# A two-layer decode kernel: the loads at the change of layers reordered, and one chunk of V more for VectorE

## The chip, the cores and the metric

The kernel runs on one core of a Trainium2 chip. The metric is the device time of one execution in microseconds (us). Three executions of the kernel before the change give a median; one further execution was recorded by the hardware profiler, and all rows below come from that one.

## The reference

One token passes twice through an attention block and an MLP, with the same weights and the same cache both times. Everything is float32.

```python
def A(x, k_cache, v_cache, wq, wo):          # D=512, 32 heads, 4096 positions, Dh=128
    q = (x @ wq).reshape(B, Sq, H, Dh).transpose(0, 2, 1, 3)
    scores = jnp.einsum("bhqd,bhkd->bhqk", q, k_cache) * (Dh ** -0.5)
    p = jax.nn.softmax(scores, axis=-1)
    o = jnp.einsum("bhqk,bhkd->bhqd", p, v_cache)
    return o.transpose(0, 2, 1, 3).reshape(B, Sq, H * Dh) @ wo

def B(x, w1, b1, w2, b2):                    # F=1376
    return jax.nn.gelu(x @ w1 + b1, approximate=True) @ w2 + b2

x = x + A(layernorm(x)); x = x + B(layernorm(x))
x = x + A(layernorm(x)); x = x + B(layernorm(x))
```

K and V of all heads are 67 MB each; layer two reads them again, less some blocks that stay on the chip from layer one.

## The kernel before, in words

**Tiling.** The 32 heads are eight groups of four (`G = 8`, `J = 4`). A group's K is one block of 8.4 MB (128 partitions x 16384 floats, eight chunks of 2048 columns, `NC`), and so is its V. Three homes of one block each in a big SBUF tile, `arena`, hold the blocks in turn (`RING` in layer one, `homes` in layer two); a smaller place, `PAIR`, takes the wo of a group and the wq of the next one (2.1 MB together). `SHARED`, inside one of the homes, takes w1 and w2 at the change of layers, and `SCRATCH` is its last 512 columns.

**Order.** Every large load is issued by SyncE's queue (`load`, line 80) in program order; one that waits for its home holds all behind it. TensorE's products are in program order too (`matmul`, line 84). A group goes: `scores` (32 products of 512 columns, which the profile counts as 64), `exponentials`, `weights`, then V. For the eleven groups that are not last or next to last in layer one nor the first two or the last in layer two, `partly` (line 379) gives the first `BY_PE` chunks of V to TensorE (`values`) and the others to VectorE (`weighted`, lines 242 and 247): one multiplication of all of them by their weights, then additions that halve the number of chunks until one is left. TensorE adds that one chunk up later (`sum_up`, line 253), at the head of the next `group`, ahead of the next scores. Behind those scores comes `out_product` with wo out of `PAIR`, and only when it has read `PAIR` may SyncE issue the next load of `PAIR`; the next K and V stand behind that load in the queue. Here is that order:

```python
        if ahead:
            t, rl, wt = ahead
            sum_up(t)
            on = head(rl)
        for c, t in k_blocks:
            scores(z, c, t)
        if ahead:
            out_product(on, wt)
```

**The change of layers.** Behind the last V of layer one comes `mlp` (line 283). Its w1 stands in four rows in `SHARED`; as each row has been used, `load_w2` puts a part of w2's eleven blocks of 512 columns over it. The last part, blocks 8 to 10, also covers `SCRATCH` and waits until line 300 has read it. After GELU the eleven blocks are multiplied one after the other (line 310), with an `idle` product (two passes of 512 columns that multiply zeros) behind blocks 1, 4, 7 and 10. Then `set_x` and `first_queries` begin layer two with the K of group 7, which is still there; wq of group 6 (`wq_t`, line 433) and the first units of group 6's K (`begin_k`) are loaded over w2's blocks, and more of that K over the chunks of `C_AT` as their scores are done. V of group 5 follows in two pieces into the same home; the second piece waits for `next_queries` of line 470.

**The end.** In layer two's last group K comes in two halves and V in four pieces; w1 and w2 go to `A_AT`, the home of the V block before, behind them in the queue.

Of the kernel before, what the change touches and what calls it, by code (L numbers as in the profile page):

```python
# [21 lines left out]
G = 8  # L22
# [3 lines left out]
FB = 11  # L26
W1C = FJ * J
EPS = 1e-5
U = 512
NC = 4 * U  # L30
# [9 lines left out]
SHARED = B_AT + KEPT_V  # L40
# [2 lines left out]
KEPT_K = PAIR + 2 * NC  # L43
ARENA = KEPT_K + U
HALVES = ((0, 4), (4, 8))
BY_PE = 3
W1_AT_END = ((0, 2), (2, 3), (3, 4))
LAST = ((0, 4), (4, 6), (6, 7), (7, 8))
W2_AT_CHANGE = ((0, 2), (2, 5), (5, 8), (8, 11))
W2_AT_END = ((0, 4), (4, 8), (8, 10), (10, 11))  # L50


# [1 line left out]
def decode_layers(ctx: ExitStack, tc: tile.TileContext, x, k, v, w, w1, b1, w2, b2, out):  # L54
# [10 lines left out]
    def small(name, n=1):  # L65
        if name not in places:
            a = sum(b - a for a, b in places.values())
            places[name] = a, a + n
        a, b = places[name]
        assert b <= 120 and b - a == n  # L70
        return smalls[:, a:b]
# [3 lines left out]
    def at(first, n):  # L75
        return arena[:, first : first + n]

    def load(first, src):
        t = at(first, src.shape[-1])
        tc.keep_in_program_order(nc.sync.dma_start(t, src))  # L80
        return t

    def matmul(*a, **kw):
        tc.keep_in_program_order(nc.tensor.matmul(*a, **kw))  # L84
# [7 lines left out]
    def of_w(row, i, n):  # L92
        return w[row][:, NC * i : NC * (i + n)]

    def by_four(t):
        return t.rearrange("p (j n) -> p j n", j=4)


    wq_t = by_four(load(SHARED, of_w(1, 0, 1)))
# [18 lines left out]
    pS, pO = (psum.tile([P, 512], F32, name=n) for n in ("pS", "pO"))  # L118
# [9 lines left out]
    def of_32(t, n, i=0):  # L128
        return t[:, : 32 * n].rearrange("p (c q) -> p c q", q=32)[:, :, i]
# [9 lines left out]
    def pairs(t):  # L139
        return t[:, :8].rearrange("p (c i) -> p c i", i=2)  # L140

    def turned(src, wide=False):

        t = work.tile([P, P], F32, name="turned")
        if wide:
            for j in range(J):
                q = slice(32 * j, 32 * j + 32)
                nc.vector.transpose(t[q], src[q, P * j : P * (j + 1)])  # L148
        else:
            nc.vector.transpose(t, src[:, :P])  # L150
        return t

    def set_x(xin0, scale, xin1, queries=True):
        s = small("x_sum")
        t = x_wide if queries else small("x1", 8)
        if not queries:
            nc.gpsimd.memset(pairs(t)[:, :, 1], 1.0)
        x = pairs(t)[:, :, 0]
        nc.vector.scalar_tensor_tensor(x, xin0, scale, xin1, op0=ALU.mult, op1=ALU.add, accum_out=s)
        if queries:  # L160
            for j in range(1, J):
                nc.gpsimd.tensor_copy(pairs(t[:, 32 * j :])[:, :, 0], x)  # L162
        return t, s

    def idle(to, n=U):
        matmul(to[:, :n], zero[:, 0:1].to_broadcast([P, P]), at(C_AT, n), start=True, stop=True)
# [6 lines left out]
    def mean_of(xs, s):  # L173
        nm = minus_mean(s, pS[:, 0:1])
        xc, sq, ss, negm = small("xc", 4), small("sq", 4), small("ss"), small("negm")
        nc.vector.tensor_scalar(xc, pairs(xs)[:, :, 0], nm, None, op0=ALU.add)
        nc.vector.scalar_tensor_tensor(sq, xc, 1.0, xc, op0=ALU.mult, op1=ALU.mult, accum_out=ss)
        nc.vector.tensor_copy(negm, nm)
        return negm, ss

    def rstd_of(ss):
        nv = minus_mean(ss, pS[:, 1:2])
        ve, r = small("ve"), small("rstd")
        nc.vector.tensor_scalar(ve, nv, -1.0, EPS, op0=ALU.mult, op1=ALU.add)
        nc.vector.memset(pS[:, 0:2], 0.0)
        nc.gpsimd.tensor_tensor(r, ve, power, op=ALU.pow)
        return r
# [43 lines left out]
    def values(i, pt, vt, c):  # L231
        for j in range(J):
            matmul(pO[32 * j : 32 * j + 4, :], pt[:, c, j, :], vt[j],
                   start=(i == 0), stop=(i == C - 1))
# [3 lines left out]
    def weighted(pt, home):  # L238
        first = home + NC * BY_PE
        t = at(first, NC * (C - BY_PE)).rearrange("p (n d) -> p n d", d=P)  # L240
        w = pt.rearrange("p c j b -> p (c j b)")[:, 4 * J * BY_PE :]
        nc.vector.tensor_tensor(t, t, w.unsqueeze(2).to_broadcast([P, 4 * J * (C - BY_PE), P]), op=ALU.mult)  # L242
        n = C - BY_PE
        while n > 1:
            m = n // 2
            a, b = at(first + NC * (n - 2 * m), NC * m), at(first + NC * (n - m), NC * m)
            nc.vector.tensor_tensor(a, a, b, op=ALU.add)  # L247
            n -= m
        return quarters(first)
# [30 lines left out]
            else:  # L280
                matmul(pO, on[:, d : d + P], wt[:, d, :], start=(d == 0), stop=(d == 3))

    def mlp(xs, s, w1_t, w2_t, load_w2=None):
        xb = small("xb", 4)
        nc.gpsimd.tensor_tensor(xb, pairs(xs)[:, :, 0], b2c, op=ALU.add)
        for c in range(4):
            for j in range(J):
                matmul(pO[32 * j : 32 * j + 2, :FJ], pairs(xs)[:, c, :], w1_t[c][:, FJ * j : FJ * (j + 1)],
                       start=(c == 0), stop=(c == 3))
            if c == 0:  # L290
                nm, ss = mean_of(xs, s)
            if c == 1:
                r = rstd_of(ss)
            if load_w2 and c < 3:
                load_w2(c)
        idle(pS)
        ht = at(SCRATCH, 32 * FB)
        nc.vector.transpose(ht, pO[:, : 32 * FB])  # L298
        h, u, a, z, t, g = (small(f"gelu_{i}", FB) for i in "huaztg")
        nc.vector.scalar_tensor_tensor(h, of_32(ht, FB, 1), nm, of_32(ht, FB), op0=ALU.mult, op1=ALU.add)  # L300
        if load_w2:
            load_w2(3)
        nc.vector.scalar_tensor_tensor(u, h, r, b1c, op0=ALU.mult, op1=ALU.add)
        nc.vector.scalar_tensor_tensor(a, u, 0.044715, u, op0=ALU.mult, op1=ALU.mult)
        nc.vector.scalar_tensor_tensor(z, a, 1.0, u, op0=ALU.add, op1=ALU.mult)
        nc.scalar.activation(t, z, AF.Tanh, scale=float(np.sqrt(2.0 / np.pi)))
        nc.vector.scalar_tensor_tensor(g, t, 1.0, u, op0=ALU.add, op1=ALU.mult)
        for c in range(FB):
            for j in range(J):
                matmul(pS[32 * j : 32 * j + 1, :P], g[:, c : c + 1], w2_t[c][:, P * j : P * (j + 1)],  # L310
                       start=(c == 0), stop=(c == FB - 1))
            if load_w2 and any(c == b - 1 for a, b in W2_AT_CHANGE):
                idle(pO)
        return of_32(turned(pS), 4), xb

    def load_w1(first, a, b):
# [2 lines left out]
    def load_w2(first, a, b):  # L319
        load(first + U * a, w2[:, U * a : U * b])  # L320

    def in_rows(first, n, rows):
        return [at(first + n * i, n) for i in range(rows)]
# [7 lines left out]
    xs, s = set_x(zero, 1.0, xcol)  # L331
# [19 lines left out]
    def next_queries(xs, negm, wt, to=pO):  # L351
        for c in range(4):
            wide_query_block(to, c, xs, wt)
        z = queries(to, negm, wide=True)
        if to is pS:
            nc.vector.memset(pS, 0.0)
        return z
# [21 lines left out]
    def partly(pt, v_blocks, home):  # L379
        for c, t in v_blocks:  # L380
            if c < BY_PE:
                values(c, pt, t, c)
# [6 lines left out]
    for g in range(G):  # L389
# [12 lines left out]
        for c, t in blocks(v, g, v_home, LAST if final else ((0, C),)):  # L402
# [3 lines left out]
            if g == G - 2:  # L406
                for j in range(J):
                    i = 4 * c + j - KEPT_V // U
# [8 lines left out]
        else:  # L417
            pair = load(PAIR, of_w(g % 2, g, 2))
            acc = add_up(acc, head_out(rl, by_four(pair[:, :NC])))
            wq_t = by_four(pair[:, NC:])  # L420
            z = next_queries(xs, negm, wq_t)
    x1, s1 = set_x(own, 1.0, acc, queries=False)
    own, xb = mlp(x1, s1, in_rows(SHARED, W1C, 4), in_rows(SHARED, U, FB),
                  lambda i: load_w2(SHARED, *W2_AT_CHANGE[i]))
    xs, s = set_x(own, 0.5, xb)


# [2 lines left out]
    g = G - 2  # L430
    negm, z, sc, nsc = first_queries(xs, s, wq_t)
    acc = pairs(xs)[:, :, 0]
    wq_t = by_four(load(SHARED, of_w((g + 1) % 2, g, 1)))
    k_t = []

    def begin_k(home, n):
        a = len(k_t)
        load(home, k[g][:, U * a : U * (a + n)])
        k_t.extend(at(home + U * i, U) for i in range(n))

    begin_k(SHARED + NC, 4)
    begin_k(SHARED + 2 * NC, 2)
    begin_k(PAIR + NC, 4)
    for c in range(C):
        scores(z, c, quarters(C_AT + NC * c))
# [27 lines left out]
    for n in range(2, G):  # L473
        g, final = G - 1 - n, n == G - 1
# [17 lines left out]
        own = head_out(rl, wo_t, last=True)  # L492
    x1, s1 = set_x(own, 1.0, acc, queries=False)
    own, xb = mlp(x1, s1, in_rows(A_AT, W1C, 4), in_rows(A_AT + 11 * U, U, FB))
    y = small("y", 4)
    nc.vector.scalar_tensor_tensor(y, own, 0.5, xb, op0=ALU.mult, op1=ALU.add)
# [43 lines left out]
```

## Time and profile before

| what | value |
|---|---|
| median of three executions | 678.74 us (677.17 to 679.43) |
| the profiled execution's own time | 680.62 us |
| its span, first to last instruction | 678.8 us |
| read from HBM | 285.88 MB, 421 GB/s over the span |
| mean granted TensorE clock | 0.796 of full speed |
| busy: TensorE, VectorE, ScalarE, GpSimd | 404.0, 333.1, 22.8, 4.3 us |

The own time is that of the execution that the profiler watched, so it holds 1.8 us outside of the span. Shares of busy time are means over stages that differ. A chain of waits, which goes back from the last instruction to what released each step, says which stage waits for what. In the rows, PE is TensorE, DVE is VectorE, ACT is ScalarE, POOL is GpSimd, and SPq is SyncE's queue; L84 is line 84.

### The profile page before, as it was taken

The numbers are of one execution on the slowest core, as the hardware profiler recorded it, in microseconds if no ns is written. First come the engines' busy times: TensorE is split into PE (matmuls) and PEld (weight loads), VectorE is DVE, ScalarE is ACT, GpSimd is POOL, SyncE is SP. The second block draws the span as 40 slices with busy tenths as digits, with TensorE's granted clock in tenths as the row PEclk, the third lists the DMA queues.
The fourth block names the chain that finished last, engine by engine and source line by source line (L and its number), as shares of the span: only waits on it lengthen the run. The fifth ranks groups of instructions, "written<-read, shape, count | busy, mean of one in ns | idle before, by whom it ended". The sixth has DMA issues, their size and how long they took to land.

```text
span 678.8 us, 5676 instructions
## 1 busy us (share of the span) xinstructions
PE 404.0 (60%) x2416; PEld 108.7 (16%) x2416; DVE 333.1 (49%) x489; ACT 22.8 (3%) x48; POOL 4.3 (1%) x21
## 2 busy tenths in 40 slices
PE   3533753638626566287688887647527465385586
PEld 1100210112101112021113222111102111121122
DVE  2059176393672936920211311295682945927622
ACT  0010000000000000001000110000000000000000
POOL 1000000000000000000000000000000000000000
PEclk9667785877759768688987998987668867778697
DMA  9999999999999999999999999999999999999996
GB/s 375 429 434 433 433 433 433 424 442 436 429 436 418 444 434 433 433 435 416 432 414 332 429 448 419 389 441 433 438 436 415 454 437 425 436 425 414 432 411 257
DMA packets 11402, 286.25 MB, mean 422 GB/s; under 512 B 1777, under 2 KB 1777, under 8 KB 3441
## 3 DMA queue, kind: packets, MB, share of 16 engines
q1 hardware_dynamic: 10944, 285.87, 98.6%
q8 instruction: 19, 0.31, 0.2%
q10 hardware_dynamic: 432, 0.01, 0.0%
q14 instruction: 7, 0.05, 0.0%
HBM read 285.88 MB, written 0.00 MB: 421 GB/s over the span
## 4 chain that ended last, share of the span: by engine, by line
DMA 57%; PE 31%; DVE 9%; issue 1%; SPq 1%; another core or an unknown queue 1%; ACT 0%; POOL 0%; DVEq 0%; ACTq 0%
DMA arena<-in_k 40%; PE pS L84 18%; PE pO L84 13%; DMA arena<-in_v 10%; DMA arena<-in_w 5%; DVE arena L242 3%; DVE arena L247 3%; DMA xcol<-in_x 1%; DVE turned L148 1%; SPq L80 1%; DVE arena L257 0%; ACT arena L214 0%; DVE ml L207 0%; DVE arena L298 0%
## 5 line engine op out<-in xcount | busy, mean ns | idle before, releaser
L84 PE MATMUL pS<-arena,zq 128*8 128x512 f32 x1024 | 136.9, 694 | 35.6 <-DMA arena<-in_k 31.7
L242 DVE TENSOR_TENSOR arena<-arena,turned 128x10240 f32<-128x10240 f32 x11 | 119.1, 10825 | 44.7 <-DMA arena<-in_v 44.7
L84 PE MATMUL pO<-arena,turned 128*4 128x512 f32 x584 | 93.3, 793 | 56.4 <-DMA arena<-in_v 54.8
L247 DVE TENSOR_TENSOR arena<-arena 128x2048 f32<-128x2048 f32 (+1 forms) x33 | 98.5, 2984 | 0.7
L84 PE MATMUL pO<-arena,one 128*4 128x512 f32 x88 | 20.8, 1037 | 127.1 <-DVE arena L247 127.1
L207 DVE TENSOR_REDUCE ml<-pS 128x1 f32<-128x512 f32 x16 | 11.1, 691 | 151.0 <-PE pS L84 151.0
L84 PE MATMUL pO<-arena,on_wide 128*128 128x512 f32 x112 | 51.8, 605 | 4.0 <-DVE on_wide L265 4.0
L84 PEld LDWEIGHTS pS<-arena,zq 128*8 128x8 f32 x1024 | 28.9, 99 | 150.4 <-issue 110.9
L84 PE MATMUL pS<-arena,x_wide 128*128 128x512 f32 x88 | 41.5, 614 | 3.6 <-DMA arena<-in_w 3.5
L257 DVE STREAM_TRANSPOSE arena<-pO 128x512 f32<-128x512 f32 x16 | 11.5, 716 | 56.3 <-PE pO L84 56.3
L84 PEld LDWEIGHTS pO<-arena,turned 128*4 128x4 f32 x584 | 16.1, 101 | 118.0 <-issue 112.4
L148 DVE STREAM_TRANSPOSE turned<-pO 32x128 f32<-32x128 f32 x72 | 22.3, 310 | 21.2 <-PE pO L84 20.4
L214 ACT ACTIVATE arena<-pS,mt,smalls 128x512 f32<-128x512 f32 x16 | 12.4, 777 | 494.9 <-DVE mt L212 494.8
L219 PE MATMUL pO<-ident,arena 128*128 128x128 f32 x64 | 10.5, 288 | 30.0 <-DVE turned L148 17.8
L84 PEld LDWEIGHTS pO<-arena,on_wide 128*128 128x128 f32 x112 | 20.1, 190 | 36.3 <-issue 29.5
L84 PE MATMUL pO<-arena,x_wide 128*128 128x512 f32 (+1 forms) x64 | 18.4, 477 | 9.5 <-POOL x_wide L162 6.7
L84 PEld LDWEIGHTS pO<-arena,one 128*4 128x4 f32 x88 | 1.2, 84 | 136.2 <-DVE arena L247 136.2
L84 PEld LDWEIGHTS pS<-arena,x_wide 128*128 128x128 f32 x88 | 16.3, 196 | 33.5 <-issue 16.9
L148 DVE STREAM_TRANSPOSE turned<-pS 32x128 f32<-32x128 f32 x44 | 13.7, 311 | 0.8
L219 PEld LDWEIGHTS pO<-ident,arena 128*128 128x128 f32 x64 | 6.8, 142 | 43.3 <-issue 27.4
L224 DVE STREAM_TRANSPOSE mt<-ml 128x32 f32<-128x32 f32 x16 | 3.4, 211 | 17.2 <-ACT arena L214 17.2
L84 PE MATMUL pO<-arena,smalls 128*2 128x344 f32 x64 | 8.2, 604 | 4.8 <-DMA arena<-in_w 4.1
(79 smaller groups left out, 121.5 us busy)
## 6 DMA issues: line engine op xcount, KB each, us to landing
arena<-in_w SPq DMA_DIRECT2D x13, 2048.0 KB, 11.5
arena<-in_k SPq DMA_DIRECT2D x4, 4096.0 KB, 24.5
arena<-in_v SPq DMA_DIRECT2D x2, 4096.0 KB, 38.4
arena<-in_w SPq DMA_DIRECT2D x6, 1024.0 KB, 20.2
arena<-in_v SPq DMA_DIRECT2D x3, 2048.0 KB, 42.8
arena<-in_v SPq DMA_DIRECT2D x1, 6144.0 KB, 26.2
arena<-in_w SPq DMA_DIRECT2D x6, 688.0 KB, 31.2
arena<-in_v SPq DMA_DIRECT2D x4, 1024.0 KB, 45.3
```

The source lines that it names most:

```text
L80: tc.keep_in_program_order(nc.sync.dma_start(t, src))
L84: tc.keep_in_program_order(nc.tensor.matmul(*a, **kw))
L148: nc.vector.transpose(t[q], src[q, P * j : P * (j + 1)])
L207: nc.vector.tensor_reduce(ml[:, 0:1], pS, axis=AX.X, op=ALU.max)
L214: nc.scalar.activation(p, pS, AF.Exp, bias=bias[:, 0:1], scale=sc, accum_out=ml[:, 0:1])
L219: tc.keep_in_program_order(nc.tensor.transpose(pT[:, b].rearrange("p j r -> p (j r)"), p[:, P * b : P * (b + 1)], ident))
L224: nc.vector.transpose(lt, ml)
L242: nc.vector.tensor_tensor(t, t, w.unsqueeze(2).to_broadcast([P, 4 * J * (C - BY_PE), P]), op=ALU.mult)
L247: nc.vector.tensor_tensor(a, a, b, op=ALU.add)
L257: nc.vector.transpose(ot, pO)
```

## The change

`BY_PE` goes from 3 to 2, so that VectorE takes six chunks of V where it took five. At the change of layers w2's last part is split into blocks 8 and 9 (issued when w1's last row has been used) and block 10 (issued behind line 300); wq is loaded in two halves behind blocks 1 and 3; the first two loads of K are issued behind blocks 7 and 9 instead of after `first_queries`; and the idle products behind blocks 1, 4, 7, 10 become idle products behind 4, 7, 9 and one of half the width behind 10.

```diff
-BY_PE = 3
+BY_PE = 2
-W2_AT_CHANGE = ((0, 2), (2, 5), (5, 8), (8, 11))
+W2_AT_CHANGE = ((0, 2), (2, 5), (5, 8), (8, 10), (10, 11))
...
-            if load_w2 and c < 3:
+            if load_w2:
                 load_w2(c)
...
         if load_w2:
-            load_w2(3)
+            load_w2(4)
...
-            if load_w2 and any(c == b - 1 for a, b in W2_AT_CHANGE):
-                idle(pO)
+            if load_w2:
+                behind_w2(c)
+                if c in (4, 7, 9):
+                    idle(pO)
+                elif c == FB - 1:
+                    idle(pO, U // 2)
...
+    def behind_w2(c):
+        if c in (1, 3):
+            load(SHARED + U * (c - 1), of_w((G - 1) % 2, G - 2, 1)[:, U * (c - 1) : U * (c + 1)])
+        if c == 7:
+            begin_k(SHARED + NC, 4)
+        if c == 9:
+            begin_k(SHARED + 2 * NC, 2)
+
     own, xb = mlp(x1, s1, in_rows(SHARED, W1C, 4), in_rows(SHARED, U, FB),
-                  lambda i: load_w2(SHARED, *W2_AT_CHANGE[i]))
+                  lambda i: load_w2(SHARED, *W2_AT_CHANGE[i]), behind_w2)
...
-    wq_t = by_four(load(SHARED, of_w((g + 1) % 2, g, 1)))
-    k_t = []
...
-    begin_k(SHARED + NC, 4)
-    begin_k(SHARED + 2 * NC, 2)
+    wq_t = by_four(at(SHARED, NC))
     begin_k(PAIR + NC, 4)
```

## Rows read from the trace of the kernel before

**Rows 1.** The chain that ended last, in order of time: start, duration, what.
```profile
354.68 6.75 DMA arena<-in_w
...
364.94 1.03 PE pS L84 x16
365.97 1.35 PE pO L84 x2
...
367.32 0.77 PE pS L84 x24
368.09 1.05 PE pO L84 x2
...
464.37 7.50 PE pS L84 x64
...
475.54 0.33 SPq L80
```

**Rows 2.** Windows: busy time by engine, granted clock, DMA share, GB/s.
```profile
366.00:370.00 4.00, 4.00 (x53) 1.90 (x54) 0.00 (x0) 0.00 (x0) 0.00 (x0) 0.93 0.67 214
...
430.00:434.00 4.00, 2.75 (x28) 0.78 (x32) 1.13 (x4) 0.00 (x0) 0.00 (x0) 1.00 0.78 287
...
475.00:610.00 135.00, 73.78 (x350) 18.53 (x348) 80.80 (x91) 2.60 (x6) 0.00 (x0) 0.73 1.00 434
610.00:614.00 4.00, 0.63 (x4) 0.42 (x4) 1.62 (x7) 0.00 (x0) 0.00 (x0) 1.00 0.77 291
```

**Rows 3.** Timeline: the last idle product and layer two's first query products.
```profile
371.66 1.13 PE L84 MATMUL pO<-arena,zero 128*128 128x512 f32 x2
...
372.72 0.62 PE L84 MATMUL pO<-arena,x_wide 128*2 128x128 f32 x16
```

**Rows 4.** DMA issues, 367.8 to 368.4 us (wq): count, KB, us to landing.
```profile
arena<-in_w SPq DMA_DIRECT2D x1, 1024.0 KB, 7.4
```

**Rows 5.** Groups by line and form: count, busy us, mean ns, idle before.
```profile
L242 DVE TENSOR_TENSOR arena<-arena,turned 128x10240 f32<-128x10240 f32 x11 | 119.1, 10825 | 44.7 <-DMA arena<-in_v 44.7
...
L247 DVE TENSOR_TENSOR arena<-arena 128x2048 f32<-128x2048 f32 x22 | 49.8, 2265 | 0.3
L247 DVE TENSOR_TENSOR arena<-arena 128x4096 f32<-128x4096 f32 x11 | 48.7, 4424 | 0.4
```

**Rows 6.** SyncE's timeline: two of ten loads of PAIR behind such groups.
```profile
126.53 0.33 SPq L80 DMA_DIRECT2D arena<-in_w  x1
...
609.90 0.33 SPq L80 DMA_DIRECT2D arena<-in_w  x1
```

**Rows 7.** Timeline: V's landing starts L242, in brackets; one group's scores.
```profile
90.07 10.82 DVE L242 TENSOR_TENSOR arena<-arena,turned 128x10240 f32<-128x10240 f32 x1 [3.42 <-DMA arena<-in_v]
...
133.65 10.82 DVE L242 TENSOR_TENSOR arena<-arena,turned 128x10240 f32<-128x10240 f32 x1 [4.71 <-DMA arena<-in_v]
...
483.42 10.82 DVE L242 TENSOR_TENSOR arena<-arena,turned 128x10240 f32<-128x10240 f32 x1 [5.47 <-DMA arena<-in_v]
...
596.40 9.84 PE L84 MATMUL pS<-arena,zq 128*8 128x512 f32 x64 [2.00 <-DMA arena<-in_k]
```

**Rows 8.** Timeline of the last such group and of the last MLP.
```profile
615.73 10.82 DVE L242 TENSOR_TENSOR arena<-arena,turned 128x10240 f32<-128x10240 f32 x1 [3.42 <-DMA arena<-in_v]
...
636.12 1.89 PE L84 MATMUL pO<-arena,one 128*4 128x512 f32 x8 [11.85 <-DVE arena L247]
637.78 7.95 PE L84 MATMUL pS<-arena,zq 128*8 128x512 f32 x64
...
664.03 0.17 DVE L159 SCALAR_TENSOR_TENSOR smalls<-turned,smalls 128x4 f32<-128x4 f32 x1
...
665.45 0.76 PE L84 MATMUL pO<-arena,smalls 128*2 128x344 f32 x8 [1.84 <-DMA arena<-in_w]
...
668.72 1.33 PE L84 MATMUL pO<-arena,smalls 128*2 128x344 f32 x8 [0.36 <-DMA arena<-in_w]
...
672.26 3.67 PE L84 MATMUL pS<-arena,smalls 128*1 128x128 f32 x88 [0.20 <-DVE smalls L307]
```

More of the change, by code (lines that the diff above doesn't have):

```diff
@@ L281, in out_product, with mlp @@
                 matmul(pO, on[:, d : d + P], wt[:, d, :], start=(d == 0), stop=(d == 3))
-    def mlp(xs, s, w1_t, w2_t, load_w2=None):
+    def mlp(xs, s, w1_t, w2_t, load_w2=None, behind_w2=None):
         xb = small("xb", 4)
@@ L422, in decode_layers, with begin_k @@
     x1, s1 = set_x(own, 1.0, acc, queries=False)
+    k_t = []
+    def begin_k(home, n):
+        a = len(k_t)
+        load(home, k[G - 2][:, U * a : U * (a + n)])
+        k_t.extend(at(home + U * i, U) for i in range(n))
+    def behind_w2(c):
[5 more added lines that the diff above has]
+            begin_k(SHARED + 2 * NC, 2)
     own, xb = mlp(x1, s1, in_rows(SHARED, W1C, 4), in_rows(SHARED, U, FB),
-                  lambda i: load_w2(SHARED, *W2_AT_CHANGE[i]))
+                  lambda i: load_w2(SHARED, *W2_AT_CHANGE[i]), behind_w2)
     xs, s = set_x(own, 0.5, xb)
@@ L432, in decode_layers @@
     acc = pairs(xs)[:, :, 0]
-    wq_t = by_four(load(SHARED, of_w((g + 1) % 2, g, 1)))
-    k_t = []
[L436 to L439, printed above, removed]
-    begin_k(SHARED + NC, 4)
-    begin_k(SHARED + 2 * NC, 2)
+    wq_t = by_four(at(SHARED, NC))
     begin_k(PAIR + NC, 4)
```

## The prediction

> **What bounds the kernel now.** I read the chain of waits first. Its long pieces are transfers of K, V and weights, so over most of the span the time is that of the bytes. Between the w1 load that lands at 361.4 us and SyncE's load at 475.54 us, though, the chain has 179 pieces and none is a transfer: GELU, w2, the queries and three attention groups run there one behind the other (its ends stand in [rows 1]). Time taken out of that stretch counts, time that a transfer saves there need not. The windows say the same from the other side: the queues move 434 GB/s at a share of 1.00 from 475 to 610 us, and the share falls to 0.67 at 366 to 370 us (the change of layers), to 0.78 at 430 to 434 and to 0.77 at 610 to 614 [rows 2]. As lost time these are 0.33 x 4 = 1.3, 0.9 and 0.9 us. Then the timelines of a middle group and of the end, for how much room there is for a slower VectorE.
>
> **The change of layers: products.** The w2 products run at 1.03 us for 16 before the clock has risen and at 0.77 for 24 after, 64 and 32 ns each [rows 1]. Now: blocks 0 and 1, an idle product of 1.35, blocks 2 to 4, then idle products of 1.05 behind blocks 4 and 7, and one more behind block 10. After: the 1.35 goes, but the part of it that ran at the low clock (its 0.3 over the full-speed 1.05) falls on blocks 2 to 4 instead, so 1.05 is saved; the new idle product behind block 9 stands ahead of block 10 and costs 1.05. Block 10 ends as before: 0. Behind it the last idle product ran from 371.66 to 372.79, and the query products began at 372.72, as it ended [rows 3]; at half the width it takes 0.5. VectorE's way to the queries is unchanged and I have it end soon after, so I take -0.4 (bounds 0 and -0.5).
>
> Fewer idle products could also cost: if the clock doesn't rise, blocks 2 to 10 (72 products) take 72 x 32 ns = 2.3 us more, and three and a half idle products twice their 1.05, 3.7 more. Ends: 0 and +6.0. Engine time before the rise is as dense as before, so I take 0. The Trainium skill speaks against this part of the change: on its page "TensorE: Matmul & The Clock Gate" (section "What's actually happening") the throttled clock is the default and only activity releases it, so that products which only keep the engine busy would be worth their time; by that the sum would be up to 6.0 us higher. The rows only show that the clock did rise here with an idle product behind block 1 (from 64 to 32 ns), not what happens without it.
>
> **The change of layers: transfers.** wq was issued at 367.9 us, behind block 3, and landed 7.4 us later [rows 4], though 1 MB takes 2.4 us at 434 GB/s; the 1.3 us of empty queue lie just there [rows 2]. After, its first half goes out behind block 1 (at 366.0 us, the end of blocks 0 and 1 [rows 1]), before the queue is empty, and w2's blocks 8 and 9 no longer wait for line 300. So the hole should close. What follows in the queue waits for products that come only 0.4 us earlier: the second piece of V waits for line 470's products at 430 us, where the share is 0.78. A queue that gets there earlier waits there longer. But 0.78 isn't 0: some of it is transfers that are behind. Of 1.3 + 0.9 = 2.2 us I take 0.4 as gained; ends 0 and 2.2. The work that hides the rest is the chain of 179 pieces; if that cover were gone it would be worth 2.2.
>
> Two loads more are issued (w2's and wq's second parts). In a filled queue they cost nothing but their bytes; each by itself could cost at most what wq's load shows, 7.4 - 2.4 = 5.0. I take 0, as both stand behind others. The Trainium skill advises batching to at least 1 MiB (page "DMA: Bandwidth & Descriptors", section "Bandwidth"), and gives a fixed cost of about 2 us a transfer (section "Anatomy of one DMA"), measured on another path than SyncE's; by that the sum would be 4 us higher. No row shows a 0.25 MB load in this place.
>
> **VectorE's sixth chunk.** The multiplication of five chunks takes 10.825 us, so six take 12.99: +2.17. Its additions are 4.424 + 2 x 2.265; six chunks are halved as three chunks, one, one. From 2048 to 4096 columns costs 2.16, so three chunks cost 6.58: again +2.16. Together +4.3 us in each of eleven groups [rows 5]. TensorE loses eight products of V, which wait for nothing and which nothing waits for: 0.
>
> Where does it surface? V lands at 90.07, the load of `PAIR` goes out at 126.53, and the next V lands at 133.65 [rows 6, 7]; the queue has work until then, a lead of 7.1 us. At 609.90 against 615.73 the lead is 5.8 [rows 6, 8]. Now the scores wait for K (2.00 us at 596.40 [rows 7]). After, they wait for `sum_up`: that began 636.12 - 615.73 = 20.4 us after V landed and will begin at 24.7; scores begin 1.7 after it, take 7.50 to 9.84 [rows 1, 7, 8], and the load follows 3.7 later (606.24 to 609.90 [rows 6, 7]). That is 37.6 to 39.9 us behind V, with V 43.6 apart (133.65 - 90.07): a lead of 3.7 to 6.0. A slip of up to two, since the wait for K absorbs the rest. I take 0 for these loads: the transfers queued cover them, and at a lead of 5.8 the loss was at most the 0.9 us at 610.
>
> One load has no such absorber. At 475.54 the chain is all products and VectorE; V lands at 483.42 [rows 1, 7], a lead of 7.9, of which 4.3 goes: 3.6. Ends 0 and about 2 (the 5.8 - 3.6 that it lacks against the lowest lead seen); I take +0.3.
>
> **The end.** In the last such group the scores don't wait for K: `sum_up` 636.12, scores 637.78 [rows 8]. All behind it moves by 4.3 until something else is later. x1 is ready at 664.2 and waits for w1 until 665.45; after, it is ready at 668.5, when w1 has landed but for a moment (the last of its four product groups began at 668.72, released by it) [rows 8]. The first w1 product would start 3.1 us later than now, and then there are no more waits for w1: four groups at 0.65 to 0.76 plus the mean's in between, 2.9 us, end at 671.4 instead of 670.05: +1.4. GELU's 2.2 us (to 672.26) follow at the same distance, so w2 begins at 673.7; 88 products at 32 ns are 2.8, against 3.67 now with waits for w2's transfers [rows 1, 8]. It ends at 676.5 instead of 675.93: +0.6. At 64 ns it would be 5.6, an end at 679.3 and +3.4. I take +0.9, near the lower end, since the engine now has its work without pauses, and with something for scores slower than 7.95.
>
> **Sum.** -0.4 - 0.4 + 0.3 + 0.9 = +0.4 against the profiled execution's 680.62 us (span 678.8 and 1.8 around it): 681.0. That execution is 1.88 above the median shown, so on the median 679.1 us.
>
> **The rivals.**
> *The hole was the bound* (faster): all 2.2 of the transfers come through, with -0.4 from the products and the end at its least, +0.6: -2.0, 676.7 us or less. For it: the queue is the bound before and after this stretch. Against: no transfer in the chain from 361 to 475 us.
> *VectorE's delay empties the queue in each group* (slower). Place: the ten loads of `PAIR`. Point: a lead under the 5.8 us at which a loss already shows [rows 2]. If each lacks on average 5.8 - 4.9 = 0.9 us, half to all of it lost, ten loads cost 4.5 to 9: 684 to 688 us. Against: the share is 1.00 over 475 to 610 us with such loads in it.
> *The end at the low clock* (slower): +3.4 in place of 0.9, 681.6 to 682. For it: the half-clock groups of 1.33 us in that MLP [rows 8].
> *The clock at the change* (slower): up to +6.0, 682 to 685 us.
> *The small loads cost by themselves* (slower): two times 2 to 5 us, 683 us and more. The page on DMA is what speaks for it; the rows don't.
> *The change does nothing measurable* is the forecast itself.
>
> **Chances.** The forecast 0.59, its own range 677.3 to 680.7; the hole 0.17; the queue emptied 0.10; the end at the low clock 0.06; the clock at the change 0.05; small loads 0.03. A measurement of this kernel tells 0.3%, 2.0 us, from no change. So faster 0.17, within 0.59, slower 0.24. The range that leaves out no more than 2 in 10 cuts the outer half of the hole (0.08) and the outer parts of the slower ones (0.12): 676.3 to 684.0.
>
> **What would show it.** Share near 1.00 at 366 to 370 us and a larger hole at 430; the first queries about 0.4 us earlier. L242 at 13.0 us, first addition 6.6. Scores directly behind `sum_up` in every group, without the wait for K, and `PAIR`'s loads 37.6 to 39.9 us behind V with the share still 1.00 from 475 to 610. At the end x1 later by 4 us against V's landing, no wait for w1, and w2's products ending about 0.6 us later. I am wrong if the time between V landings grows over 43.6, if the hole at 430 doesn't grow, or if w2's last products run at 64 ns.

## The result, and the profile after

The changed kernel takes **682.15 us** (median of 22 runs, 679.73 to 685.0) against **679.17** for the kernel before, run beside it (22 runs, 677.17 to 681.48). The ratio is **1.0043, with a 95% interval of 1.0031 to 1.0054**: slower by 2.9 us (2.1 to 3.7). The forecast of 679.1 was "no measurable change". Its range, up to 684.0, holds the time, but in the part that was there for the slower rivals. The profiled execution of after took 683.47 us (span 681.7), against 680.62 (678.8) before.

First the groups of instructions of after, by line and form (count, then busy us, mean ns of one, idle before and what ended it):

```profile
L242 DVE TENSOR_TENSOR arena<-arena,turned 128x12288 f32<-128x12288 f32 x11 | 142.5, 12958 | 30.5 <-DMA arena<-in_v 30.4
L84 PE MATMUL pS<-arena,zq 128*8 128x512 f32 x1024 | 130.4, 667 | 16.4 <-DMA arena<-in_k 12.6 <-DVE zq L197 3.3 <-DVE pS L185 0.5
...
L247 DVE TENSOR_TENSOR arena<-arena 128x6144 f32<-128x6144 f32 x11 | 72.1, 6558 | 0.4
```

VectorE's work costs what was worked out from [rows 5]: 12.96 us for the multiplication (13.0 forecast), 6.56 for the first addition (6.58). Its own wait for V has fallen from 44.7 to 30.5 us, so of 11 x 4.3 = 47 us of new work only some 14 came out of waiting for V; the rest pushes back what follows. Scores wait 12.6 us for K in the whole execution, 31.7 before: the absorber of the prediction is mostly used up.

Then the windows of after (busy time by engine, granted clock, DMA share, GB/s), against [rows 2]:

```profile
366.00:370.00 4.00, 3.94 (x68) 1.73 (x56) 0.00 (x0) 0.00 (x0) 0.00 (x0) 1.00 0.98 390
430.00:434.00 4.00, 2.36 (x19) 0.55 (x21) 1.48 (x5) 0.00 (x0) 0.00 (x0) 1.00 0.77 283
475.00:610.00 135.00, 69.29 (x351) 18.86 (x344) 93.97 (x89) 2.60 (x6) 0.00 (x0) 0.77 1.00 424
```

The hole at the change of layers is closed (214 GB/s before, 390 now), as foreseen, and the one at 430 us is no larger, as far as windows of 4 us tell (the last section). But over 475 to 610 us the queues move 424 GB/s where they moved 434: 135 x (1 - 424/434) = 3.1 us (1.9 against the 430 GB/s of the kernel below that has the change of layers alone). The share reads 1.00 in both, so it is the rate that tells. Where it went, the chain that ended last shows (start, us, what):

```profile
443.52 12.97 DVE arena L242
...
468.18 1.89 PE pO L84 x8
...
470.06 7.38 PE pS L84 x64
477.45 3.65 PE pO L84 x8
481.11 0.33 SPq L80
...
481.96 47.43 DMA arena<-in_v
...
529.57 12.97 DVE arena L242
```

In the first group of layer two that VectorE works on (n = 2) its product begins at 443.52, `sum_up` at 468.18, 24.7 us later (20.4 before), the scores follow, and SyncE can issue the load of `PAIR` at 481.11 only, 5.6 us later than the 475.54 of [rows 1]. Behind that load stand K and V. The timeline has what that does:

```profile
439.69 0.33 SPq L80 DMA_DIRECT2D arena<-in_v  x1
...
481.11 0.33 SPq L80 DMA_DIRECT2D arena<-in_w  x1
...
483.56 12.96 DVE L242 TENSOR_TENSOR arena<-arena,turned 128x12288 f32<-128x12288 f32 x1
...
529.57 12.96 DVE L242 TENSOR_TENSOR arena<-arena,turned 128x12288 f32<-128x12288 f32 x1 [5.42 <-DMA arena<-in_v]
```

The view of DMA issues has the time from the issue at 439.69 to that V's landing:

```profile
arena<-in_v SPq DMA_DIRECT2D x1, 43.6
```

From here on "lead" is the time from the issue of a `PAIR` load to the landing of the V that is then under way. Where L242 waits for that V, it starts 0.1 to 0.5 us after the landing and stands for it; here its line has no bracket, so it waited for VectorE's own steps, and V had landed before, at 439.69 + 43.6 = 483.3 us. The lead was 7.8 us here (7.9 to the start of L242 [rows 1, 7]), was forecast at 3.6, and is 2.1. The next V lands 46.1 us after this one, where 43.6 was the beat before [rows 7]: 2.5 us lost at one load. The eight others of middle groups in this trace have leads of 4.5 to 7.7.

At the end of after, in the timeline:

```profile
641.90 1.89 PE L84 MATMUL pO<-arena,one 128*4 128x512 f32 x8 [13.26 <-DVE arena L247]
643.56 7.79 PE L84 MATMUL pS<-arena,zq 128*8 128x512 f32 x64
...
669.65 0.17 DVE L159 SCALAR_TENSOR_TENSOR smalls<-turned,smalls 128x4 f32<-128x4 f32 x1
...
669.88 0.76 PE L84 MATMUL pO<-arena,smalls 128*2 128x344 f32 x8 [0.65 <-DVE smalls L159]
...
674.90 1.05 PE L84 MATMUL pS<-arena,smalls 128*1 128x128 f32 x32 [1.16 <-DVE smalls L307]
676.41 1.05 PE L84 MATMUL pS<-arena,smalls 128*1 128x128 f32 x32 [0.46 <-DMA arena<-in_w]
677.64 1.04 PE L84 MATMUL pS<-arena,smalls 128*1 128x128 f32 x24 [0.18 <-DMA arena<-in_w]
```

w1's products no longer wait for w1 but for x1 (1.84 us of waiting for a transfer in [rows 8]; here 0.65 us, and for VectorE). The last products of w2, though, wait for transfers twice: the queue, late by then, is the end again.

### The profile page after: what moved, and what is told of

Its sections match the earlier page's. It is cut to its first block, busy times and chain, and to the rows that moved or that the text cites. A ratio compares the mean times of both kernels' runs of the same rounds, so it can differ in the third digit from the quotient of the medians.

```text
span 681.7 us, 5508 instructions
## 1 busy us (share of the span) xinstructions
PE 382.2 (56%) x2328; PEld 106.5 (16%) x2328; DVE 380.2 (56%) x489; ACT 22.8 (3%) x48; POOL 4.3 (1%) x21
## 5 line engine op out<-in xcount | busy, mean ns | idle before, releaser
L242 DVE TENSOR_TENSOR arena<-arena,turned 128x12288 f32<-128x12288 f32 x11 | 142.5, 12958 | 30.5 <-DMA arena<-in_v 30.4
L84 PE MATMUL pS<-arena,zq 128*8 128x512 f32 x1024 | 130.4, 667 | 16.4 <-DMA arena<-in_k 12.6
L247 DVE TENSOR_TENSOR arena<-arena 128x2048 f32<-128x2048 f32 (+1 forms) x33 | 122.0, 3696 | 0.7
L84 PE MATMUL pO<-arena,turned 128*4 128x512 f32 x496 | 78.3, 779 | 42.1 <-DMA arena<-in_v 40.1
L84 PE MATMUL pS<-arena,x_wide 128*128 128x512 f32 x88 | 48.4, 700 | 21.0 <-DMA arena<-in_w 21.0
L84 PEld LDWEIGHTS pS<-arena,x_wide 128*128 128x128 f32 x88 | 18.7, 224 | 59.0 <-DMA arena<-in_w 36.9
L84 PEld LDWEIGHTS pO<-arena,turned 128*4 128x4 f32 x496 | 12.9, 97 | 88.6 <-issue 84.2
L84 PEld LDWEIGHTS pO<-arena,x_wide 128*128 128x128 f32 (+1 forms) x64 | 6.8, 145 | 18.3 <-POOL x_wide L162 6.7
## 6 DMA issues: line engine op xcount, KB each, us to landing
arena<-in_k SPq DMA_DIRECT2D x4, 4096.0 KB, 24.7
```

## The experiments

Two theories stood at the start. **Late loads**: VectorE's 4.3 us come out where a load of `PAIR`, issued behind `sum_up`, scores and softmax, finds the queue running empty, and K and V behind it come late. **Change of layers**: the new order of the small loads costs, and VectorE's chunk is covered. The first four expectations split the first theory in two: "two places" (it costs in n = 2 and n = 6 alone) and "everywhere" (each of the eleven groups pays). Each ratio below is against the kernel before on the same chip (its median there 678.6 to 679.2 us), with its 95% interval; it is estimated from all runs, so it can differ by about 0.1% from the quotient of the two medians. All kernels compute the whole reference.

**The two parts apart.** The change of layers alone, in the kernel after:

```diff
-BY_PE = 2
+BY_PE = 3
```

> The change of layers is changed, VectorE keeps five chunks. Theory 'two places' (the cost of the change sits in the sixth chunk, in the group after the change of layers and in the last such group of layer two): no slower than before, 0 to 1.5 us faster, since the second piece of V after the change landed at the same time (439.65 against 439.72 us) though the trace was 1.4 us late ahead of it. Rival 'layers' (the reordered loads cost): 2 to 3 us slower, as the whole change. Rival 'everywhere' (each of the eleven groups pays): like two places here.

Measured: 678.92 us, **1.0000 (0.9986 to 1.0014)**. The chunk alone, in the kernel before:

```diff
-BY_PE = 3
+BY_PE = 2
```

> VectorE takes six chunks in all eleven groups, the change of layers is as before. Two places: 3 to 4.5 us slower than before. Everywhere: the same, 3 to 4.5. Layers: 0 to 1 us slower.

Measured: 681.94 us, **1.0048 (1.0031 to 1.0066)**. The chunk is the whole loss, and "change of layers" falls.

**In which groups.** `partly` and `weighted` take the number of TensorE's chunks as an argument, so that each group has its own. The first two:

```diff
-    def weighted(pt, home):
+    def weighted(pt, home, BY_PE):
-    def partly(pt, v_blocks, home):
+    def partly(pt, v_blocks, home, BY_PE):
...
-            t = partly(pt, blocks(v, g, v_home), v_home)
+            t = partly(pt, blocks(v, g, v_home), v_home, 3)
```

and in layer two's call `2 if n in (2, G - 2) else 3`: the whole change, but six chunks only in n = 2 and n = 6.

> The whole change, but VectorE takes six chunks in two groups alone: the first one after the change of layers and the last one of layer two; five in the other nine. Two places: 2 to 3 us slower than before, nearly the whole change's 2.9. Everywhere: two elevenths of 3 to 4.5 us on top of the layers' part, so between 0.5 slower and 0.5 faster than before.

Measured: 680.48 us, **1.0027 (1.0015 to 1.004)**.

The reverse, 2 in layer one and `3 if n in (2, G - 2) else 2` in layer two, is six chunks in the other nine groups.

> The whole change, but VectorE takes five chunks in the first group after the change of layers and in the last one of layer two; six in the other nine. Two places: 1 us faster to 0.5 slower than before. Everywhere: 1.5 to 3 us slower than before.

Measured: 680.29 us, **1.0029 (1.0015 to 1.0043)**. Both halves cost, some 2 us each. So "two places" falls too, as does "everywhere" with equal shares (1.8 us for two groups, 2.0 for nine), and the loads that I had at nothing aren't free. Where it lies in the nine groups the trace hardly says, as the profiled execution (678.89 us) was the fastest of this kernel's twelve, 1.4 us under their median. Its timeline's end has one late load:

```profile
608.66 0.33 SPq L80 DMA_DIRECT2D arena<-in_w  x1
...
612.76 10.82 DVE L242 TENSOR_TENSOR arena<-arena,turned 128x10240 f32<-128x10240 f32 x1 [1.68 <-DMA arena<-in_v]
...
663.56 0.76 PE L84 MATMUL pO<-arena,smalls 128*2 128x344 f32 x8 [2.26 <-DMA arena<-in_w]
```

A load with a lead of 4.1 us, and w1 ready 663.56 - 612.76 = 50.8 us behind V's landing, where it was 665.45 - 615.73 = 49.7 [rows 8]: 1.1 us late. All V's of layer two before it land on the old beat.

**Single groups.** Layer two's n = 2, n = 5 and n = 6 alone, and layer one's six alone, each with the new change of layers:

```diff
-    2 if n in (2, G - 2) else 3
+    2 if n == 2 else 3
+    2 if n == 5 else 3
+    2 if n == G - 2 else 3
+    3
```

(one of the four lines each; layer one's call has 3 in the first three and 2 in the last).

> The whole change, but VectorE takes six chunks in one group alone, the first that it works on after the change of layers (n = 2). Theory 'late load' (the sixth chunk costs only where SyncE's next load of PAIR then goes out under about 5 us ahead of V's landing, and the queue behind it starts late and slowly): 1.5 to 2.2 us slower than before, all of it around the load at 481 us, with V to V 45.5 to 46 us there instead of 43.6. Rival 'each group pays the same' (3.3 us over eleven groups): 0.3 us, lost in the spread.

Measured: 679.88 us, **1.0018 (1.0005 to 1.0031)**. Its timeline and a window of it:

```profile
480.08 0.33 SPq L80 DMA_DIRECT2D arena<-in_w  x1
...
482.53 10.82 DVE L242 TENSOR_TENSOR arena<-arena,turned 128x10240 f32<-128x10240 f32 x1
...
527.61 10.83 DVE L242 TENSOR_TENSOR arena<-arena,turned 128x10240 f32<-128x10240 f32 x1 [4.76 <-DMA arena<-in_v]
```

```profile
479.00:481.00 2.00, 1.05 (x3) 0.19 (x1) 1.70 (x8) 0.10 (x2) 0.00 (x0) 1.00 0.02 4
```

Again L242 did not wait for V, which was issued at 437.08, took 44.3 us and landed at 481.4: the lead is 1.3 us. Hardly a packet starts (4 GB/s) in the last microsecond before the load and the first behind it, and the next V lands 46.1 us later instead of 43.6. One group of eleven, and 1.2 us by the ratio (0.3 to 2.1).

> The whole change, but six chunks in one group alone, the one ahead of the load of PAIR at 610 us (n = 5). Late load: 0.8 to 1.2 us slower than before, with the load at 610 landing 5.7 to 6.2 us behind V instead of 4.9. Each group the same: 0.3 us.

Measured: 679.12 us, **1.0004 (0.999 to 1.0019)**. A miss for the late-load theory as I had sized it:

```profile
609.68 0.33 SPq L80 DMA_DIRECT2D arena<-in_w  x1
...
614.04 10.82 DVE L242 TENSOR_TENSOR arena<-arena,turned 128x10240 f32<-128x10240 f32 x1 [1.95 <-DMA arena<-in_v]
...
663.77 0.76 PE L84 MATMUL pO<-arena,smalls 128*2 128x344 f32 x8 [1.59 <-DMA arena<-in_w]
```

A lead of 4.4 us, and w1 comes 663.77 - 614.04 = 49.7 us behind V, as before. With 4.1 us it was 1.1 late, with 4.4 not at all; in one execution each that is within what a V shows by itself (the last section).

> The whole change, but six chunks in the six groups of layer one alone, five in layer two. 'Late load': 0 to 0.4 us slower than before, since the loads of PAIR of layer one kept leads of 4.4 to 7 us with six chunks and V still landed every 43.6 us. 'Each group pays the same' (1.9 us over the nine): 1.2 us slower.

Measured: 678.78 us, **1.0005 (0.999 to 1.002)**. Layer one's six groups cost nothing that can be measured, though the rival's 1.2 us lies within the interval too.

> The whole change, but six chunks in the last such group of layer two alone (n = 6). The end as predicted (its chain moves by 4.3 us and most of that lies under the wait for w1): 0.3 to 1 us slower than before, 0.6 from the difference of the runs with two groups and with n = 2 alone; less where the clock rises early in the scores, more where late. Each group the same: 0.2 to 0.3 us.

Measured: 678.99 us, **1.0000 (0.9986 to 1.0013)**. Its timeline at the end:

```profile
641.39 7.56 PE L84 MATMUL pS<-arena,zq 128*8 128x512 f32 x64
...
672.51 2.83 PE L84 MATMUL pS<-arena,smalls 128*1 128x128 f32 x88 [1.16 <-DVE smalls L307]
```

w2's last products run almost without a pause from 672.51, in 2.83 us where [rows 8] had 3.67, and end at 675.34, where they ended at 675.93 before; V's landing was 0.66 earlier too (615.07), so the end stands where it stood. With the loads before it in time, no cost of the last group's chunk shows (-1.0 to 0.9 us).

**The wait taken away.** If the wait in front of K and V is the cause, half of `PAIR`'s load can go out before it and K not stand behind it. The wq half is issued right behind V, then K; wo's half goes out behind K, in the fifth chunk of the next scores:

```diff
-            t, rl, wt = ahead
+            t, rl, load_wo = ahead
+            if ahead and c == 4:
+                wt = by_four(load_wo())
-            pair = load(PAIR, of_w(g % 2, g, 2))
-            ahead = t, rl, by_four(pair[:, :NC])
+            wq_t = by_four(load(PAIR + NC, of_w(g % 2, g + 1, 1)))
+            ahead = t, rl, lambda g=g: load(PAIR, of_w(g % 2, g, 1))
```

(layer one; layer two with the halves the other way round). With six chunks:

> The whole change with six chunks everywhere, but the load of PAIR is split for the eleven groups: the wq half goes out as soon as the last queries have read it, K next, and only the wo half and V wait for the product with wo. Nothing is taken out; the wait for that product no longer holds K. Late load: the loss of the whole change goes, 0.5 us slower to 1.5 faster than before, no hole at 481 and 610 us. Each group the same, or VectorE's streaming slowing the transfers themselves: still 2.5 to 3.5 us slower, since the work of VectorE is the same.

Measured: 680.09 us, **1.0023 (1.0011 to 1.0034)**, 1.6 us slower: between the two forecasts, and a miss for both. With five:

> The changed layers, five chunks, and the split load. Late load: 0 to 1.5 us faster than before, about what the load at 610 lost there (0.5 us of empty queue) and the small dips at the other loads. If it is no faster than the change of layers alone, the leads of the kernel before were long enough.

Measured: 679.13 us, **1.0004 (0.9988 to 1.0019)**. Splitting alone gains nothing that can be measured: with five chunks the leads were long enough. And six chunks in ten groups, five in the last:

> The split load with six chunks in ten groups, five in the last one (n = 6). If what was left with the split load and six chunks (1.6 us) was the end: 0 to 0.7 us slower than before. If VectorE's longer work costs by itself in each group: still 1.2 to 1.6 us slower.

Measured: 679.51 us, **1.0007 (0.9994 to 1.0021)**. In its timeline:

```profile
483.11 12.96 DVE L242 TENSOR_TENSOR arena<-arena,turned 128x12288 f32<-128x12288 f32 x1 [0.20 <-DMA arena<-in_v]
...
526.86 12.96 DVE L242 TENSOR_TENSOR arena<-arena,turned 128x12288 f32<-128x12288 f32 x1 [2.66 <-DMA arena<-in_w]
```

526.86 - 483.11 = 43.75 us: the beat of before, though VectorE has its sixth chunk in n = 2. Ten groups with six chunks cost 0.5 us (-0.4 to 1.4) this way, against 3.3 (2.1 to 4.5) for eleven with the joint load, and the eleventh by itself was measured at 0. These intervals don't touch: most of the loss is the load that waits with K and V behind it, not VectorE's time as such. (The joint load with these ten groups was not run.)

The kernel with all eleven groups says it less clearly: 1.6 us (0.7 to 2.3), half of the joint load's loss, with intervals that just overlap. In its profiled execution the next V in the same place lands 45.2 us behind, but without a gap in the queue (the table below). Its timeline ends so:

```profile
641.17 9.05 PE L84 MATMUL pS<-arena,zq 128*8 128x512 f32 x64
...
673.78 2.58 PE L84 MATMUL pS<-arena,smalls 128*1 128x128 f32 x88 [1.16 <-DVE smalls L307]
```

No wait for a transfer is left there, the scores took 9.05 us (7.56 with n = 6 alone), and w2 began 1.3 us later than in that kernel. Whether the rest of its loss is at this end isn't settled.

**Fewer idle products still.** The change of layers without the chunk, with the idle products behind blocks 4 and 7 alone:

```diff
-BY_PE = 2
+BY_PE = 3
-                if c in (4, 7, 9):
+                if c in (4, 7):
                     idle(pO)
-                elif c == FB - 1:
-                    idle(pO, U // 2)
```

> The changed layers with five chunks, and idle products behind blocks 4 and 7 alone: those behind 9 and 10 are left out. If the idle product behind block 9 gave back what the dropped one saved: the first queries come 1.3 to 1.6 us earlier against GELU than in the kernel before, the clock stays high, and the time is 0.3 to 1.3 us shorter than before. Rival 'clock': without them the clock falls in the queries and the first scores take up to 14 us instead of 7.1: 1 to 4 us slower.

Measured: 678.28 us, **0.9986 (0.997 to 1.0002)**, the fastest of all, its interval just over 1. Two lines of its timeline, and its windows:

```profile
364.46 1.27 PE L84 MATMUL pS<-arena,smalls 128*1 128x128 f32 x40 [1.10 <-DVE smalls L307]
...
370.02 0.62 PE L84 MATMUL pO<-arena,x_wide 128*2 128x128 f32 x16 [0.64 <-DVE x_wide L159]
```

```profile
366.00:370.00 4.00, 3.38 (x52) 1.33 (x50) 0.49 (x3) 0.00 (x0) 0.00 (x0) 1.00 1.06 378
370.00:380.00 10.00, 9.36 (x115) 3.15 (x116) 2.16 (x12) 0.00 (x0) 0.99 (x4) 1.00 1.00 413
```

From w2's first product to the first query product 370.02 - 364.46 = 5.6 us, against 372.72 - 364.94 = 7.8 before [rows 1, 3]. The granted clock is 1.00, the 2.4 GHz level, from 366 to 380 us without the two idle products. Not all of the difference is theirs: blocks 0 to 4 (40 products) took 1.27 us here, 32 ns each, so the clock was up before w2 began, where the kernel with this part alone took 1.94 (below). And the queries wait 0.64 us for VectorE behind block 10, about as long as the idle product of half the width took there, so leaving that one out gave back next to nothing.

## Why the prediction failed, step by step

**What bounds the kernel.** Right: transfers, and two stretches in which products and VectorE set when loads go out. What was read wrong was the slack between them.

**The change of layers, products (-0.4).** Right, and with the mechanism. In the timeline of the kernel with this part alone:

```profile
365.00 1.94 PE L84 MATMUL pS<-arena,smalls 128*1 128x128 f32 x40 [0.16 <-DVE smalls L307]
...
370.29 1.12 PE L84 MATMUL pO<-arena,zero 128*128 128x512 f32 x2
371.34 0.40 PE L84 MATMUL pS<-arena,smalls 128*1 128x128 f32 x8
...
372.39 0.62 PE L84 MATMUL pO<-arena,x_wide 128*2 128x128 f32 x16
```

From w2's first product to the queries 7.39 us instead of 7.78. The idle product at 370.29, behind block 9, stands ahead of block 10 and gives back the 1.05 that was saved; in the kernel without it, above, block 10 follows block 9 at once, and of the 7.39 - 5.56 = 1.83 us between the two 0.67 are the earlier clock and 1.05 this product. The clock rose within blocks 0 to 4 (40 products in 1.94 us, 49 ns each, between the 64 and 32 of [rows 1]), without the idle product behind block 1. The rival "clock at the change" is out. The rule cited from the Trainium skill (page "TensorE: Matmul & The Clock Gate", section "What's actually happening"), that the clock is throttled until activity releases it, isn't contradicted: the clock did rise, with fewer idle products. The 6.0 us that I had worked out for that rule didn't come.

**The change of layers, transfers (-0.4).** The hole closed, and nothing that can be measured came of it: 1.0000 (0.9986 to 1.0014) for the whole part, -0.8 forecast; the interval is 1.0 us wide to either side and can't tell -0.8 from 0. "The hole was the bound" (-2.0) is out. So are the small loads, since the whole part costs nothing. The Trainium skill's page "DMA: Bandwidth & Descriptors" (section "Anatomy of one DMA") gives a fixed cost of about 2 us for a transfer on GpSimd's path; the 4 us for two loads more were an estimate worked out from it, and behind others in SyncE's queue it doesn't show here (0.0, -1.0 to 1.0).

**VectorE's chunk: the loads (0, and +0.3). This is the step that failed.** "I take 0 for these loads: the transfers queued cover them." The mechanism was in the prediction, as a rival with 0.10 and as the upper end (2) of the one load at 475 us; its size was wrong, in four ways, and its own sign, "if the time between V landings grows over 43.6", came. (1) The load at 475 us: +1.2 us (0.3 to 2.1) instead of 0.3. Its lead fell by 5.6 us in after, not by 4.3: the group itself began 1.4 later (L242 at 443.52, 442.09 before), and V landed no later. With six chunks in n = 2 alone it fell by 6.5: the group began 1.2 earlier, but its scores took 9.2 us instead of 7.7, and V landed 1.9 earlier. (2) The nine others outside n = 2 and 6: 2.0 us (1.0 to 2.9), taken at 0. (3) The price was looked for in the share of 475 to 610 us, which can't show it: it reads 1.00 before, 1.00 after, with 10 GB/s between them. (4) The prediction had it that "the queue has work until then", that is until V lands. But with n = 2 alone hardly a packet starts after 479.0, and V lands at 481.4: by that trace the queue has nothing left to start some 2.4 us before the landing, so a lead of 3.6, as forecast, is worth an estimated 1.2.

The rival as I priced it, ten loads with an equal loss, was wrong as well: at 4.5 to 9 us it is too dear, and the loss is not equal. It sits where the lead is least:

```
kernel                               lead   next V   GB/s, 470 to 496 us   ratio
five chunks in n=2: layers only       7.3    43.6           432            1.0000
six in n=2, joint load: n=2 only      1.3    46.1           378            1.0018
  n=2 and 6                           1.0    46.1           401            1.0027
  chunk only                          2.4    45.0           407            1.0048
  after                               2.1    46.1           404            1.0043
six in n=2, split load: all eleven    2.3    45.2           424            1.0023
  not in n=6                          2.5    43.7           440            1.0007
```

(One profiled execution each, the load at 475 to 482 us. "Next V" is from landing to landing. With the split load the lead is that of wo's half, and K has stood in the queue for 12 us by then.) The rates stand in windows like these, of before, after, n = 2 alone and the split load with all eleven, in this order:

```profile
470.00:496.00 26.00, 15.42 (x64) 4.54 (x56) 16.58 (x18) 0.87 (x2) 0.00 (x0) 0.80 1.01 437
...
470.00:496.00 26.00, 18.89 (x104) 5.86 (x92) 17.61 (x20) 0.87 (x2) 0.00 (x0) 0.85 0.98 404
...
470.00:496.00 26.00, 18.83 (x99) 5.59 (x88) 17.48 (x18) 0.87 (x2) 0.00 (x0) 0.89 0.90 378
...
470.00:496.00 26.00, 16.07 (x91) 4.77 (x80) 17.68 (x18) 0.87 (x2) 0.00 (x0) 0.89 0.99 424
```

All four kernels with six chunks in n = 2 and the joint load have leads of 1.0 to 2.4, move 378 to 407 GB/s here and lose 1.4 to 2.5 us on the next V. The ten other kernels move 419 to 440. With each packet of the traces spread over its own time, the four fall short of 434 GB/s by 2.1 to 2.3 us of transfers from 476 to 490 us, the ten by at most 0.3. Among the ten are the two with the split load, whose late half goes out just as late: with K already queued, a short lead leaves no gap. At leads of 4.1 and 4.4 the ends above lost 1.1 and 0, in one execution each.

**The end (+0.9).** x1 came 5.6 us later, w1's wait went, and w2's products began 2.6 later instead of 1.4, as V was 1.5 later too. The mechanism was right and the term probably too high: the last group's chunk alone measures 0.0 (-1.0 to 0.9). The pauses that w2's products had for transfers take the delay up. In after the late load makes the transfers late again. "The end at the low clock" is out: no run with six chunks there had it.

**The sum.** Measured apart, n = 2, n = 6 and the other nine come to 1.2 + 0.0 + 2.0 = 3.2 us; the chunk in all eleven is 3.3, the whole change 2.9. So the parts add up, within intervals of about 1 us each. I had +1.2 for these (0.3 + 0.9) and -0.8 for the change of layers. That the range, up to 684.0, holds 682.15 is luck: its upper part was there for slower rivals, of which the end at the low clock (681.6 to 682), the clock at the change (682 to 685) and the small loads (683 and more) did not come, and the one that did come was priced at 684 to 688.

**What stays open.** Where the 2.0 us of the nine groups lie. Layer one's six are 0.3 us (-0.7 to 1.4), n = 5 is 0.3 (-0.7 to 1.3), which leaves some 1.4 for n = 3 and n = 4, not tried alone, with an uncertainty as large. That late loads are the cause there is shown only in so far as splitting the load took most of the whole loss away. A sum of small losses is as possible as one place. Whether the 0.14% of the kernel with two idle products is a gain isn't settled either.

## What to carry to other kernels

Work added to an engine that is "only" 49% busy is paid for where a load is issued behind it: list, for every load, how long before the queue runs dry it goes out, and take the added time off each lead, with what the stages before it can slip; here leads of 1.0 to 2.4 us to V's landing cost 1 to 2 us, and leads of 7 to 8 nothing. When a lead gets too short, don't take work off the engine first: see what waits in the queue behind the load that is late, and let it go ahead (splitting one load in two took out half of the loss or more). And an idle product costs its own length wherever it stands ahead of work on the path that is ready; leave it out once and read the granted clock.

## What the hardware showed beside it

**Windows of a few us mislead on transfers.** In the middle of a queue that is never empty, windows of after read:

```profile
538.00:542.00 4.00, 0.02 (x1) 0.00 (x0) 4.00 (x1) 0.00 (x0) 0.00 (x0) 1.00 1.21 524
542.00:546.00 4.00, 0.00 (x0) 0.00 (x0) 3.96 (x2) 0.00 (x0) 0.00 (x0) 0.58 0.72 311
```

So a share of 0.77 in 4 us, on which I had put 0.9 us of lost time twice [rows 2], is within the scatter. A share of 1.21 can't be a busy time: a window counts each packet whole where it starts, and one of 64 KB takes 2.4 us (the median in the trace before). For the same reason a stand-still such as 4 GB/s says that no packet starts, not that none is under way. What can be trusted are the distances between landings and rates over longer stretches: over 26 us the ten kernels without a late load scatter from 419 to 440 GB/s.

**One V in an execution can be 1.5 us late by itself.** In the kernel with six chunks at n = 6 alone, the timeline has

```profile
474.98 0.33 SPq L80 DMA_DIRECT2D arena<-in_w  x1
...
482.76 10.83 DVE L242 TENSOR_TENSOR arena<-arena,turned 128x10240 f32<-128x10240 f32 x1 [5.37 <-DMA arena<-in_v]
...
527.97 10.82 DVE L242 TENSOR_TENSOR arena<-arena,turned 128x10240 f32<-128x10240 f32 x1 [4.24 <-DMA arena<-in_v]
```

a lead of 7.8 us, and yet 45.2 us to the next V. The kernel before has such a distance too, 45.1 us from 526.99 to 572.12; so have the one with six chunks in n = 5 alone (45.2 between landings, behind the V of 525.36) and the split load with all eleven (45.2, in the table). They come at other places in other executions, the queue moves its full rate meanwhile (440 GB/s from 470 to 496 us in the kernel shown here), and I know no cause. A loss of 1.5 us in one trace is thus no proof, and the chunk-only kernel's 1.4 alone could be such a one. The reading above rests on four of four at the same place, three of them at 2.5 us, on the lower rate that goes with it in these four alone, and on the time of the kernel that has only this group.
